# An mLSTM cell followed by a gated two-layer block: a reordered head (later gates, third weighed k, w_in's second quarter, sine's table)

## The chip, the cores and the metric

The kernel runs on one core of a Trainium2 chip. The metric is device time in microseconds (us) of the whole program. The core has five engines that run their own instruction lists in order and wait for one another by semaphores: PE (TensorE, matmul), DVE (VectorE), ACT (ScalarE), POOL (GpSimd) and SP (SyncE, here the engine that issues most DMAs). A profile names an instruction by its line in the kernel ("L528") and its tiles ("qG<-t,G"). Times "at 40.03" are us from the start of the profiled span.

## What is computed

Two stages. The first is an mLSTM cell for 4 batches and 8 heads, 768 steps, head size 40:

```
m_new  = max(f_gate + m, i_gate)
C      = exp(f_gate + m - m_new) * C + exp(i_gate - m_new) * outer(v, k)
n      = exp(f_gate + m - m_new) * n + exp(i_gate - m_new) * k
y[t]   = sigmoid(o_gate) * (C @ q) / max(|n . q|, 1)
```

The second takes the 3072 rows of 320 values that the first gives (8 heads side by side) as x:

```
h   = x @ w_in          (320 x 2048, float64 in memory)
g   = h * cos(h)
out = g @ w_out         (2048 x 320, float64 in memory)
```

All work is in float32. The float64 weights are brought down to float32 in the kernel.

## The kernel before

**Cells.** The sequence is cut into 6 chunks of 128 steps, and a cell n is one chunk of one batch (c, b = divmod(n, 4)), 24 in all. Within a chunk the recurrence is written as a masked product: E holds the decays between two steps (loaded as running maxima from a DRAM table M_d, masked and put through exp), `scores` makes k.q on PE, `weigh` multiplies by E on DVE, `values` multiplies by v on PE. What comes from earlier chunks is a state per batch (`st`), which `values` adds as qG times st, where qG is q scaled by the carry G (loaded by `load_G` or `load_G_of` from a DRAM table G_d). The 4 cells of chunk 0 (n = 0 to 3) have no carry.

**Second stage.** For each chunk c, 8 slots f2 of 256 columns of w_in: `Up(c, f2)` makes h on PE in two PSUM banks "pup" (L725 for the last 64 rows of x, L731 for the other 256), then h*cos(h) by `near` (ACT L739), `rest` (DVE L742), `sin` (ACT L747, which needs the sine table in ACT) and `gate` (DVE L751, tile g). `down` multiplies g by w_out (PE L845, tile po). Up(0, 0) and Up(0, 1) use the first quarter of w_in's columns, Up(0, 2) and Up(0, 3) the second.

**Weights.** A piece of float64 weight comes as pairs of words into a place of the tile `blocks` (w_in: four DMAs L163 of 128 KB, or four L216 of 64 KB for the last rows) or into `bits` (w_out: one DMA L222 of 640 KB). It is brought down by `take_apart` (ACT L175, L177), `bound` (DVE L181, L182), `join` (DVE L191) and `round_up` (POOL L195); `put_together` is the last two. A quarter of w_in is three pieces: two of 512 columns and a last one, w_in_l.

**Order.** The order is written out by hand under a manual schedule: an engine's list is the order of the calls. `first_cells` is the head: the gates, cells 0 to 3, w_in's first quarter and what cell 4 (n = B) needs; `first_period` is slots 0 and 1 of chunk 0 with cell 4; after that `both_parts` runs two slots and one cell at a time. Each engine's list is strictly in order, and so is SP's list of DMA issues. A DMA issue on SP also waits for the landing of the DMA eight issues before it, since eight completion semaphores go round.

**The later gates** (chunks 1 to 5) are made in the head: `gates_sums` (DVE L288), `gates_less_sums` (POOL L291 to L293), `gates_maxima` (DVE scan L296, then POOL issues the DMA to M_d, L298), `gates_exponents` (POOL L301 to L304), `gates_exp` (two ACT exps L308, then POOL issues two DMAs to G_d, L311), `gates_turn` (PE L322, ACT L323 into the table `tab`), `gates_diagonal`, `gates_spread` and `gates_keep` (ACT L332).

**Other places the change touches.** `weigh_k(n)` is POOL L469, k times a gate, into a tile kw of which there are two; cells 2 and 3 reuse the places of cells 0 and 1, which PE reads in `seam` (L683). `load_M(n)` is L424, the masking of E is `decay_exponents` (POOL L450), its exp is `decay` (ACT L464, 8 instructions from cell 4 on). `turn_blocks` (DVE L524) turns q and k for cells from 4 on, `scale_q` is qG (POOL L528), `odd_constants` fills the tile vr (POOL L138, L139) and `odd_values_of` copies a part of v into it (POOL L506). In `values(4)` PE runs, in this order, L572 and L581 (E and qG), again L572 and L581, then L575 and L578 (vr) and L581. `state(n)` copies or adds the state (ACT L706 for n < 4). `warm` gives PE matmuls of zeros.

Of the kernel before, what the change touches and what calls it, by code (L numbers as in the profile page):

```python
# [29 lines left out]
def kernel(  # L30
# [23 lines left out]
    C = 128  # L54
# [138 lines left out]
    def round_up(dst, bits):  # L193
        t = dst.bitcast(I32)
        nc.gpsimd.tensor_tensor(out=t, in0=t, in1=bits[:, 0:dst.shape[1], 0], op=OP.add)  # L195
# [94 lines left out]
    def gates_less_sums():  # L290
        nc.gpsimd.tensor_tensor(out=a1, in0=a1, in1=F1, op=OP.subtract)  # L291
        nc.gpsimd.tensor_copy(out=shift[:, 0, 0:1], in_=F0[:, last])
        nc.gpsimd.tensor_copy(out=shift[:, 1:R, 0:1], in_=F1[:, 0:R - 1, last])  # L293
# [37 lines left out]
    def gates_keep(pd):  # L331
        nc.scalar.copy(out=tab[:, 1:R, 3], in_=pd)  # L332
# [132 lines left out]

    def weigh_k(n):
        if n < N - B:
            kw = p2.tile([128, H, D], FP, name="kw", tag="kw")
            nc.gpsimd.tensor_tensor(out=kw, in0=ks(n)[:, :, 0:D], in1=cols(n, 1, D), op=OP.mult)  # L469
            kws[n] = kw  # L470

# [14 lines left out]
    def turn(n):  # L486

        pool, tag = psum(n)
        pts[n] = []
        for src in (qs(n), ks(n)):  # L490
            pt = pool.tile([128, HP, C], FP, name="pt", tag=tag)
            for p in range(HP):
                nc.tensor.transpose(pt[:, p], pair(src, p), ident)
            pts[n].append(pt)
        qkT[n] = [p1.tile([128, HP, C], FP, name=f"t{i}", tag=f"t{i}") for i in range(2)]
# [58 lines left out]
    def values(n):  # L554
        pool, tag = psum(n)
        E = Es[n]
        if n < B:
            ph = pool.tile([128, H, D1], FP, name="ph", tag=tag)
            for j in range(2):
                for p in range(HP):  # L560
                    h = 2 * p + j
                    nc.tensor.matmul(ph[:, h], E[:, h], vs(n)[:, h, 0:D1], start=True, stop=True)
            heads_of[n] = ph
            return
        vt = pool.tile([128, 4, C], FP, name="vt", tag=tag)
        state = st[n % B]

        for i in range(3):
            if i < 2:
                for a in range(HP):  # L570
                    h = 2 * a + i
                    nc.tensor.matmul(vt[32 * a:32 * a + 32, i], vs(n)[:, h, 0:32], E[:, h], start=True, stop=False)  # L572
            else:
                for a in range(HP):
                    nc.tensor.matmul(vt[32 * a:32 * a + 32, i], vr2[n // 2 % 2][:, n % 2, a, 1:3].rearrange("q g d o -> q (g d o)"),  # L575
                                     E[:, 2 * a + 1], start=True, stop=False)
                for a in range(HP):
                    nc.tensor.matmul(vt[32 * a:32 * a + 16, i], vr2[n // 2 % 2][:, n % 2, a, 0].rearrange("q d o -> q (d o)"),  # L578
                                     E[:, 2 * a], start=False, stop=False)
            for a in range(HP):  # L580
                nc.tensor.matmul(vt[32 * a:32 * a + 32, i], state[:, ts(HP * i + a, 32)], Gs[n][:, a], start=False, stop=True)  # L581
        heads_of[n] = vt
# [502 lines left out]
    def less_sums(n):  # L1085
        for i in range(2):
            decay_exponents_half(n, i)

    def first_cells():
        gates_in()  # L1090
        nc.scalar.copy(out=ident_b, in_=ident)
        for i in range(3):
            r = ts(i, BH)
            nc.scalar.copy(out=of_parts[r], in_=ident[r, r])
        load(0, "qk")
        gates_constants()
        ones_of_values()
        later_gates_in()
        load(0, "v")
        load(1, "qk")  # L1100
        load_o(0)
        load(1, "v")
        load(2, "qk")
        warm(9)
        wall_in(0, 0, pmu)
        gates_first()
        for n in range(B):
            load_E(n)
        load(2, "v")
        load(3, "qkv")  # L1110
        maxima_in_parts()
        gates_first_out()
        wall_in(0, 1, psum_o())
        for i in range(2):
            spread(0, i)
        for i in range(2):
            decay_exponents_half(0, i)
        turn(0)
        turn_out(0, False)
        decay(0)  # L1120
        maxima_in(1)
        less_sums(1)
        weigh_k(0)
        blocks_constants()
        weigh_k(1)
        state_constants()
        scores(0)
        turn(1)
        decay(1)
        turn_out(1, False)  # L1130
        weigh(0)
        sigmoid_next()
        sigmoid(0)
        exp_next()
        gates_sums()
        gates_less_sums()
        values(0)
        pieces.extend(weights_in(0))
        scores(1)
        weigh(1)  # L1140
        maxima_in(2)
        less_sums(2)
        decay(2)
        values(1)
        normalize(0)
        maxima_in(3)
        less_sums(3)
        turn(2)
        turn_out(2, False)
        weigh_k(2)  # L1150
        seam(0)
        gates_maxima()
        gates_exponents()
        load_M(B)
        load_blocks(B)
        load(B, "kv")
        outs.append((0, weights_out(0)))
        load_blocks(B + 1)
        seam_out(0)
        scores(2)  # L1160
        decay(3)
        state(0)
        weigh(2)
        turn(3)
        normalize(1)
        turn_out(3, False)
        weigh_k(3)
        values(2)
        take_apart(*pieces[0])
        seam(1)  # L1170
        normalize(2)
        scores(3)
        seam_out(1)
        bound(pieces[0][0])
        take_apart(*pieces[1])
        seam(2)
        weigh(3)
        values(3)
        join(*pieces[0])
        round_up(*pieces.pop(0))  # L1180
        seam_out(2)
        gates_exp()
        load_G_of(B)
        state(2)
        more = weights_in(1)
        pieces.append(next(more))
        take_apart(*pieces[1])
        normalize(3)
        gates_turn()
        warm(3, psum_o())  # L1190
        bound(pieces[0][0])
        put_together(*pieces.pop(0))
        pieces.append(next(more))
        load_M(B + 1)
        seam(3)
        seam_out(3)
        bound(pieces[0][0])
        put_together(*pieces.pop(0))
        state(1)
        gates_diagonal()  # L1200
        decay_exponents(B)
        pieces.extend(more)
        load_G_of(B + 1)
        load(B + 1, "kv")
        outs.append((1, weights_out(1)))
        load_o(1)
        outs.append((2, weights_out(2)))
        low_dimensions(B)
        turn_blocks(B)
        state(3)  # L1210
        decay(B)
        scale_q(B)
        weigh_k(B)
        odd_constants()
        odd_values_of(B)
# [18 lines left out]
    def first_period():  # L1234
        n = B
        up = Up(0, 0)
        scores(n)
        pd = gates_spread()
        warm(8, psum_o())
        for e in range(2):  # L1240
            up.near(e)
        gates_keep(pd)
        for e in range(2):
            up.rest(e)
        weigh(n)
        for e in range(2):
            up.sin(e)
            up.gate(e)
        values(n)
        seam(n)  # L1250
        p, piece = outs.pop(0)
        take_apart(*piece)
        low_dimensions(n + 1)
        for some in pieces:
            take_apart(*some)
        out_of_psum(n)
        on_vector([piece])
        up = Up(0, 1)
        turn_blocks(n + 1)
        on_vector(pieces)  # L1260
        pieces.clear()
        more = weights_in(2)
        pieces.append(next(more))
        load_M(n + 2)
        pieces.extend(more)
        load_blocks(n + 2)
        load_out(p)
        for e in range(2):
            up.near(e)
        for e in range(2):  # L1270
            up.rest(e)
        for e in range(2):
            up.sin(e)
            up.gate(e)
        p, piece = outs.pop(0)
        take_apart(*piece)
        denominators(n)
        fade(n)
        decay_exponents(n + 1)
        on_vector([piece])  # L1280
        state(n)
        odd_values_of(n + 1)
        down_slot(0, 1)
        sigmoid(1)
        decay(n + 1)
        divide(n)
        scale_q(n + 1)
        weigh_k(n + 1)
        load_G(n + 2)
        load_two(n + 2)  # L1290
        load_out(p)
        load_M(n + 3)
# [257 lines left out]
```

## Time and profile before

| what | value |
|---|---|
| median of 3 runs | 514.73 us (512.44 to 516.18) |
| the profiled execution | 514.64 us, span 512.9 us, so 1.74 us lie around the span |
| granted PE clock, mean | 0.993 |
| busy share | PE 97%, DVE 81%, ACT 63%, POOL 59% |
| PE's gaps over 0.04 us up to 41 us | 0.99, 0.51, 0.13, 0.21, 0.76 us |
| PE's gaps from 41 to 103 us | 0.64, 0.30, 0.54, 0.05, 0.47, 1.39, 0.52, 0.32 us |
| PE's gaps from 103 to 446 us | 0.19, 0.16, 1.06, 1.10, 0.17, 0.26, 0.41, 0.14 us |

How to read it: a line of a timeline has the start, the duration, the engine, the line of code, the operation, the tiles and shapes, and a count where like instructions were merged; in brackets stand the idle time of that engine before it and what ended that wait. A line of the table of stretches has busy time of each engine, then the granted PE clock (1.00 is full), the mean busy share of the 16 DMA engines and what they moved in GB/s. The trace also has the time at which each DMA's completions came in.

### The profile page before, as it was taken

To read this page: it belongs to the slowest core of one execution; us is meant where nothing else is said; L and a number is where in the kernel's file an instruction comes from. 1 tells how busy PE (TensorE), PEld (TensorE's weight loads), DVE (VectorE), ACT (ScalarE), POOL (GpSimd) and SP (SyncE) were. 2 spreads that over 40 slices of the span, in tenths; PEclk is the share of its full clock that TensorE was granted. 3 is DMA by queue.
4 is the path that set the end of the run, shared out by engine and by line. 5 is a ranking of instruction groups with operands and counts; after the bars stand their busy time and mean duration, and the time that the engine had idled before them with its cause. 6 is when DMAs were issued, how large, how long until landed. Compare 5 with 4: busy or idle time off the path is not lost.

```text
span 512.9 us, 11085 instructions
## 1 busy us (share of the span) xinstructions
PE 498.3 (97%) x4034; PEld 376.8 (73%) x4034; DVE 417.6 (81%) x840; ACT 325.2 (63%) x622; POOL 302.8 (59%) x390
## 2 busy tenths in 40 slices
PE   8999998999999999999999999999999999999996
PEld 6765554555675776688888688878778878787876
DVE  7887898986788887889987979998979967677655
ACT  6769779667953657747757858558858654444541
POOL 8443856544825955857576868566767455534340
PEclk9979999999999999999999999999999999999999
DMA  9978989898157527208729106828102000010001
GB/s 136 189 198 197 269 178 279 206 228 164 60 144 140 143 57 151 83 32 189 175 61 186 42 31 169 174 77 174 59 33 82 4 5 6 2 52 0 1 0 54
DMA packets 100583, 56.80 MB, mean 111 GB/s; under 512 B 63472, under 2 KB 93248, under 8 KB 100528
## 3 DMA queue, kind: packets, MB, share of 16 engines
q1 hardware_dynamic: 97408, 54.43, 45.3%
q10 hardware_dynamic: 2752, 1.23, 1.0%
q8 instruction: 32, 0.52, 0.4%
q0 software_dynamic: 368, 0.43, 0.3%
q14 instruction: 23, 0.19, 0.1%
HBM read 50.66 MB, written 4.10 MB: 107 GB/s over the span
## 4 chain that ended last, share of the span: by engine, by line
PE 73%; DVE 8%; DMA 6%; ACT 4%; SPq 3%; POOL 3%; issue 2%; DVEq 0%; ACTq 0%; POOLq 0%
PE acc L995 22%; PE pup L799 16%; PE pup L731 7%; PE pup L815 6%; PE late L995 4%; PE ps L546 4%; PE po L845 3%; PE pup L725 2%; PE vt L581 2%; PE vt L572 2%; DVE t L524 1%; PE pu L683 1%; DMA blocks<-in_moe_w_in_dram 1%; DVE n L742 1%; DMA ks<-in_k_dram 1%
## 5 line engine op out<-in xcount | busy, mean ns | idle before, releaser
L739 ACT ACTIVATE n<-pup 128x512 int32<-128x512 f32 x64 | 37.0, 594 | 95.9 <-DVE pup L824 64.7
L747 ACT ACTIVATE n<-n 128x512 f32<-128x512 f32 x96 | 58.2, 627 | 22.5 <-DVE n L742 16.2
L834 POOL TENSOR_TENSOR g<-g,n 128x512 f32<-128x512 f32 x31 | 39.6, 1276 | 52.2 <-ACT n L747 50.8
L742 DVE SCALAR_TENSOR_TENSOR n<-pup,n 128x512 f32<-128x512 f32 x64 | 43.1, 689 | 23.3 <-ACT n L739 20.8
L731 PE MATMUL pup<-xT,w_in_sb 128*128 128x512 f32 x128 | 59.2, 605 | 2.0 <-DVE g L751 2.0
L995 PE MATMUL acc<-w_out_sb,g 128*128 128x160 f32 x320 | 58.4, 302 | 0.0
L816 POOL TENSOR_TENSOR blocks<-blocks 128x256 f32<-128x256 f32 x32 | 25.7, 802 | 52.4 <-ACT blocks L808 52.4
L995 PE MATMUL acc<-T,g 128*128 128x160 f32 x304 | 55.8, 301 | 0.0
L799 PE MATMUL pup<-xT,w_in_sb 128*128 128x256 f32 x192 | 53.1, 385 | 0.4 <-ACT blocks L808 0.2
L464 ACT ACTIVATE E<-E,tab 128x128 f32<-128x128 f32 x160 | 50.2, 391 | 3.9 <-POOL E L450 3.7
L995 PEld LDWEIGHTS acc<-w_out_sb,g 128*128 128x128 f32 x320 | 49.0, 190 | 4.5 <-issue 2.7
L751 DVE TENSOR_TENSOR g<-pup,n 128x512 f32<-128x512 f32 x64 | 42.6, 687 | 7.5 <-ACT n L747 6.9
L731 PEld LDWEIGHTS pup<-xT,w_in_sb 128*128 128x128 f32 x128 | 23.3, 191 | 33.2 <-issue 31.1
L995 PEld LDWEIGHTS acc<-T,g 128*128 128x128 f32 x304 | 46.0, 190 | 0.9 <-issue 0.4
L799 PEld LDWEIGHTS pup<-xT,w_in_sb 128*128 128x128 f32 x192 | 33.8, 189 | 9.7 <-ACT blocks L808 5.9
L799 PE MATMUL pup<-x_room,room 128*128 128x256 f32 x128 | 38.2, 380 | 0.0
L824 DVE TENSOR_TENSOR pup<-pup,blocks 128x256 f32<-128x256 f32 x32 | 13.9, 436 | 29.2 <-PE pup L815 26.0
L807 ACT COPY blocks<-pup 128x512 f32<-128x512 f32 x32 | 18.6, 580 | 29.5 <-PE pup L799 27.8
L845 PE MATMUL po<-w_out_sb,g 128*128 128x320 f32 x128 | 36.3, 436 | 1.0 <-POOL w_out_sb L195 1.0
L528 POOL TENSOR_TENSOR qG<-t,G 128x512 f32<-128x512 f32 x20 | 25.9, 1295 | 18.7 <-DVE t L524 16.8
L995 PE MATMUL acc<-T,blocks 128*128 128x160 f32 x160 | 36.2, 308 | 0.0
L815 PE MATMUL pup<-xL,w_in_l 64*128 64x512 f32 x128 | 36.1, 641 | 0.0
(219 smaller groups left out, 1219.6 us busy)
## 6 DMA issues: line engine op xcount, KB each, us to landing
E<-M_d SPq DMA_DIRECT2D x20, 512.0 KB
qr<-in_q_dram SPq DMA_DIRECT2D x72, 80.0 KB
kr<-in_k_dram SPq DMA_DIRECT2D x72, 80.0 KB
bits<-in_moe_w_out_dram SPq DMA_DIRECT2D x8, 640.0 KB
G<-G_d SPq DMA_DIRECT2D x18, 256.0 KB
blocks<-in_moe_w_in_dram SPq DMA_DIRECT2D x32, 128.0 KB
out_dram<-o_sb SPq DMA_DIRECT2D x23, 160.0 KB
o<-in_o_gate_dram SPq DMA_DIRECT2D x40, 80.0 KB
```

The costliest lines, as they stand in the source:

```text
L464: nc.scalar.activation(out=Es[n][:, h], in_=Es[n][:, h], func=AF.Exp, scale=-1.0, bias=tab[:, c, 0, g:g + 1])
L528: nc.gpsimd.tensor_tensor(out=qG, in0=qkT[n][0], in1=Gs[n], op=OP.mult)
L731: nc.tensor.matmul(pu.rearrange("p (b t) -> p b t", b=B), w_in_sb[:, i, ts(2 * f2 + e, 128)], xT[c][:, i:NK * B:NK], start=(i == 0 and not ...
L739: nc.scalar.activation(out=self.n[e], in_=self.pu[e], func=AF.Copy, bias=0.25)
L742: nc.vector.scalar_tensor_tensor(out=self.n[e].bitcast(FP), in0=self.pu[e], scalar=0.25, in1=self.n[e], op0=OP.add, op1=OP.subtract)
L747: nc.scalar.activation(out=r, in_=r, func=AF.Sin, scale=TWO_PI_DOWN)
L751: nc.vector.tensor_tensor(out=g, in0=self.pu[e], in1=self.n[e].bitcast(FP), op=OP.mult)
L799: nc.tensor.matmul(bank[:, part].rearrange("p (b t) -> p b t", b=B // 2), w[:, f2], x, start=start, stop=stop, skip_group_check=True)
L815: nc.tensor.matmul(pu, w_in_l[r, f2], xL[c][r].rearrange("p b t -> p (b t)"), start=False, stop=True, skip_group_check=True)
L834: tt(out=self.g, in0=self.g, in1=self.n[e].bitcast(FP), op=OP.mult)
L845: nc.tensor.matmul(po[c][b], gs[c, f][:, ts(b, C)], w_out_sb[:, f], start=(f == 0), stop=(f == NF - 1))
L995: nc.tensor.matmul(a, lhs, rhs, start=start, stop=stop)
```

## The change

Nothing is computed differently; one tile gets another place and calls change their order in the head.

- `weigh_k(2)` writes to a place of its own (the place that o_gate's raw tile has later) and is called right after `gates_less_sums`; before, it came after `turn_out(2)`.
- `gates_maxima` and `gates_exponents` are called before `less_sums(3)`, `turn(2)` and `turn_out(2)`.
- `gates_exp` is called before `seam(2)`; before, it came after `seam_out(2)`, join and round_up of w_in's first piece.
- On SP's list: w_out's second piece (640 KB) is issued right after `load_blocks(B + 1)`; then w_in's second quarter's first two pieces and `load_M(B + 1)`; then `load_G_of(B)`, which before stood ahead of all of these.
- `decay_exponents(B)` comes right after the first piece's round_up, and `bound` of the second piece ahead of `normalize(3)`.
- `state(1)` comes ahead of `seam(3)`; `state(3)` moves from `first_cells` into `first_period`, after `gates_keep`, and `gates_keep` moves from before `rest` to after the two sines.
- `sin_next` (the load of ACT's sine table) is called after `decay(B)`, ahead of `Up(0, 0)`'s nears.

```diff
     def weigh_k(n):
         if n < N - B:
-            kw = p2.tile([128, H, D], FP, name="kw", tag="kw")
+            if n == 2:
+                kw = p1.tile([128, B, 2 * C // 32, D], FP, name="kw_o", tag="o")[:, 0]
+            else:
+                kw = p2.tile([128, H, D], FP, name="kw", tag="kw")
...
         exp_next()
         gates_sums()
         gates_less_sums()
+        weigh_k(2)
         values(0)
...
         normalize(0)
         maxima_in(3)
-        less_sums(3)
-        turn(2)
-        turn_out(2, False)
-        weigh_k(2)
-        seam(0)
         gates_maxima()
         gates_exponents()
         load_M(B)
         load_blocks(B)
+        less_sums(3)
+        turn(2)
+        turn_out(2, False)
+        seam(0)
         load(B, "kv")
         outs.append((0, weights_out(0)))
         load_blocks(B + 1)
+        outs.append((1, weights_out(1)))
         seam_out(0)
...
         take_apart(*pieces[1])
+        gates_exp()
         seam(2)
         weigh(3)
         values(3)
         join(*pieces[0])
         round_up(*pieces.pop(0))
+        decay_exponents(B)
         seam_out(2)
-        gates_exp()
-        load_G_of(B)
         state(2)
         more = weights_in(1)
         pieces.append(next(more))
         take_apart(*pieces[1])
+        bound(pieces[0][0])
         normalize(3)
         gates_turn()
         warm(3, psum_o())
-        bound(pieces[0][0])
+        state(1)
         put_together(*pieces.pop(0))
         pieces.append(next(more))
         load_M(B + 1)
+        load_G_of(B)
         seam(3)
         seam_out(3)
         bound(pieces[0][0])
         put_together(*pieces.pop(0))
-        state(1)
         gates_diagonal()
-        decay_exponents(B)
         pieces.extend(more)
         load_G_of(B + 1)
         load(B + 1, "kv")
-        outs.append((1, weights_out(1)))
         load_o(1)
         outs.append((2, weights_out(2)))
         low_dimensions(B)
         turn_blocks(B)
-        state(3)
         decay(B)
+        sin_next()
         scale_q(B)
...
         for e in range(2):
             up.near(e)
-        gates_keep(pd)
         for e in range(2):
             up.rest(e)
         weigh(n)
         for e in range(2):
             up.sin(e)
             up.gate(e)
+        gates_keep(pd)
+        state(B - 1)
         values(n)
```

## The prediction

> **What bounds the kernel now.** I read the page first, then the timelines of the five engines from 0 to 108 us, SP's waits, and tables of stretches.
>
> ```profile
> PE 498.3 (97%) x4034; PEld 376.8 (73%) x4034; DVE 417.6 (81%) x840; ACT 325.2 (63%) x622; POOL 302.8 (59%) x390
> ...
> PEclk9979999999999999999999999999999999999999
> DMA  9978989898157527208729106828102000010001
> ```
>
> PE carries the time. The DMA engines are 70 to 90% busy in the head (a slice is 12.8 us), and PE's clock falls only there. From 103 us to 446 us PE idles 3.5 us in all, so a change to the head is worth what it moves PE by at about 102 us. What can be won there is PE's idle from 41 to 103 us, 4.2 us, or 0.8%.
>
> ```profile
> 43.33 0.43 PE L572 MATMUL vt<-E,vs 128*32 128x128 f32 x8 [0.64 <-issue]
> 44.34 0.40 PE L575 MATMUL vt<-E,vr 128*32 128x128 f32 x8
> ...
> 79.72 3.67 PE L731 MATMUL pup<-xT,w_in_sb 128*128 128x512 f32 x8 [1.39 <-DVE g L751]
> ...
> 84.98 1.16 PE L546 MATMUL ps<-t,t 40*128 40x128 f32 x16 [0.52 <-DVE t L524]
> ...
> 102.10 3.67 PE L731 MATMUL pup<-xT,w_in_sb 128*128 128x512 f32 x8 [0.32 <-DVE g L751]
> ```
>
> These waits are small and end on DVE: between 45 and 85 us ACT and DVE are nearly as full as PE. ACT's own two waits there are the ones the change aims at, w_in's second quarter and o_gate:
>
> ```profile
> 50.15 0.46 ACT L175 ACTIVATE w_in_l<-blocks 128x256 f32<-128x256 f32 x1 [0.61 <-DMA blocks<-in_moe_w_in_dram]
> ...
> 57.73 1.28 ACT L372 ACT_TABLE_LOAD   x1 [1.68 <-DMA o<-in_o_gate_dram]
> ```
>
> Both come from SP's list, which waits 3.0 us (SP's waits) for G_d ahead of the carry G, while the DMA engines run dry (share 0.15 below):
>
> ```profile
> 31.99 0.86 SPq L393 DMA_DIRECT2D kr<-in_k_dram  x2
> 35.90 1.15 SPq L516 DMA_DIRECT2D G<-G_d  x2
> 37.22 3.71 SPq L163 DMA_DIRECT2D blocks<-in_moe_w_in_dram  x8
> 40.97 0.42 SPq L424 DMA_DIRECT2D E<-M_d  x1
> ```
>
> **The change part by part.**
>
> *Maxima, exponents, third k.* L296 (1.53) starts at 17.4, not 18.62. POOL's 5.47 us wait before L469 goes, so M_d is issued at 19.0 instead of 20.62 and L304 ends at 22.8 instead of 24.38; the fourth k then waits for nothing. M_d landed at 24.64, before SP's issues of w_in_l end at 25.07, so the read of it gains at most SP's wait of 0.3; I take 0. The cost: E(3)'s exp on ACT goes from 19.34 to 20.2, and with it `turn_out(3)` to 23.0; ACT's idle of 1.67 before 23.80 hides it, uncovered it is 0.9.
>
> *Later gates' exps.* L308 (1.36) moves into ACT's idle of 2.00 before 28.68, so `seam_out(2)` is not later. G_d is issued at 27.4, not 30.74, lands near 32, and SP's 3.0 us wait is gone.
>
> *Pieces, mask, sine table.* `bound` (0.9) moves into DVE's idle of 1.56 before 30.92; E(4)'s mask (1.09) into POOL's idle of 2.22 before 34.07. The second round_up ends at 34.4 instead of 35.35, but Up(0, 0) started at 34.35 behind `seam(3)`, of which nothing moves, and did not wait: 0. E(4)'s exp goes from 38.24 to 35.45, the table load (1.28) falls beside Up(0, 0), and near moves from 40.71 to 39.6, so sin, g and the 0.64 wait at 43.33 come 1.1 us sooner or go. `state(3)` (0.75) lands on ACT at 42.4 between sin and w_out's pieces; ACT won 1.1 there, net 0.
>
> *SP's list.* This decides. Behind kr at 32.85 now stand, in order, w_out's second piece (655 KB), eight issues of w_in (1049 KB), E(5) from M_d (524 KB), and only then G for cell 4 (262 KB), which used to be first. Landings come in SP's order in the trace. The rates:
>
> ```profile
> 26.00:28.00 2.00, 2.00 (x18) 1.45 (x16) 1.82 (x4) 0.68 (x2) 0.44 (x1) 0.50 0.86 252
> 35.00:37.00 2.00, 2.00 (x5) 0.76 (x4) 1.93 (x5) 1.79 (x8) 0.93 (x2) 0.93 0.15 41
> 39.00:44.00 5.00, 4.36 (x50) 2.54 (x50) 2.55 (x5) 4.95 (x12) 3.27 (x7) 1.00 0.90 231
> 52.00:54.00 2.00, 2.00 (x9) 1.38 (x8) 2.00 (x4) 0.85 (x2) 1.06 (x1) 1.00 1.04 366
> ```
>
> These are E, the dry stretch, w_in and w_out, in GB/s in the last column. From 35.3, when kr is through: w_out 655/366 = 1.8, w_in 1049/245 = 4.3 (231 here, 258 in the stretch 59 to 64), E 524/260 = 2.0, G 262/260 = 1.0, and 0.4 to the last completion: 44.8. The eighth-before rule does not add: G's two issues go when the second and third w_in pieces have landed, near 40. So w_in_l lands at 46.5 instead of 50 and o_gate near 52 instead of 57.6, and both ACT waits go; but G lands at 44.8 instead of 40.0.
>
> POOL stands at qG with all that is queued behind it:
>
> ```profile
> 40.03 1.27 POOL L528 TENSOR_TENSOR qG<-t,G 128x512 f32<-128x512 f32 x1 [1.82 <-DMA G<-G_d]
> 41.25 0.73 POOL L469 TENSOR_TENSOR kw<-ks,tab 128x320 f32<-128x320 f32 x1
> ...
> 43.17 0.24 POOL L506 COPY vr<-vs 128x64 f32<-128x64 f32 x1
> ```
>
> From qG's start to vr's end are 3.38, say 3.5 with DVE busy beside it. PE, in order, needs qG for L581 and vr for L575: it stands from 42.9 to 46.1 and again to 48.3, where before L575 ran at 44.34. From L575 to the end of Up(0, 1) are 5.84 (44.34 to 50.18), so 54.1 instead of 50.18: 3.9 later. How much survives: from 50.18 to 84.98 PE took 34.80, of it waits 0.30 + 0.54 + 0.05 + 0.47 + 1.39 + 0.52 = 3.3 and some 0.6 in a low product of 1.72 at 67.94 (1.13 elsewhere). Without waits that is 30.9, so 3.9 is given back and PE reaches 84.98's place at 85.0: +0.05. DVE and ACT are not later than that: with 5.84 after 48.3, sigmoid starts 3.4 after PE's end (near, rest, sin 1.95, w_out's take_apart 1.47) at 57.5, against 57.73.
>
> *The clock.* The stall has a second price.
>
> ```profile
> 21.60:25.00 3.40, 2.44 (x30) 2.08 (x31) 3.23 (x11) 1.73 (x4) 2.78 (x4) 1.00 0.86 257
> 25.10:28.40 3.30, 3.30 (x32) 2.65 (x28) 3.02 (x7) 1.57 (x4) 0.93 (x1) 0.50 0.72 211
> 28.50:31.80 3.30, 3.30 (x46) 3.04 (x43) 1.67 (x6) 3.10 (x10) 2.31 (x3) 1.00 0.96 195
> 31.90:35.20 3.30, 3.30 (x26) 1.95 (x24) 2.98 (x7) 1.74 (x8) 1.13 (x1) 0.50 0.91 302
> ```
>
> Stretches of 3.4 us with short matmuls, one of them without a gap, are followed by 3.4 us at half clock. From 42.6 to 49 PE would have about 1.5 us of short matmuls. I take half clock until about 52.3, by when Up(0, 1) has run 3 us: 1.5 us. Bounds: 0 if the clock stays, 3.4 if two stretches of Up and po run at half. The Trainium skill, page "TensorE: Matmul & The Clock Gate", section "The HAM clock gate (the "warmup" mystery)", has the clock fall after an idle window of about 3.4 us; by that the matmuls inside the stall keep it up, and the 1.5 goes (third rival). The row 28.50 to 31.80 disagrees: no idle, and half clock after it.
>
> **Sum.** +0.05 + 1.5 - 0.32 (the wait at 102.10 is absorbed) = +1.2, on the profiled 514.64, which stands 0.09 under the median of the runs: 515.8. With G between 43.9 and 46 and the clock's loss from 0.8 to 2.5 it is 514.2 to 518.
>
> **Rivals.**
>
> *G is not late enough to matter (faster).* If all 2490 KB move at w_out's 366 GB/s, G lands at 35.3 + 6.8 + 0.4 = 42.5, L575 runs at 46.0, PE is 2.25 earlier at 84.98 and the clock may hold: 512.4. For it: w_in rows of 258 at full share, and ACT's slack of 1.68. Against: w_in never ran over 312 in any us of the head. The Trainium skill, page "DMA: Bandwidth & Descriptors", section "Bandwidth", measures 341 GB/s for 1 MB; by it, as an estimate, G's data would be through at 42.6 and the time near this rival's. The w_in rows of 231 and 258 speak against that rate here.
>
> *G is very late (slower by over 1%).* If the stream behind w_out runs at the 163 GB/s of 46 to 50 us, G lands at 35.3 + 1.8 + 1835/163 + 0.4 = 48.8: PE +4.0, clock +1.5, less 0.32: 519.8. It decides from a landing past 48.5. Against: that stretch held 160-byte rows of k and v, which now come after G.
>
> *The stall comes, the clock stays full.* 514.64 + 0.05 - 0.32 = 514.4.
>
> *The change does nothing.* The gates sooner hide behind `seam(3)` and G's delay stays small enough: 514.6, inside the case before.
>
> **How the numbers follow.** Forecast (stall and half clock) 0.53; full clock or nothing 0.18; G early 0.20; G very late 0.06; not foreseen 0.03. A measurement of this kernel tells about 1% (5.1 us) from no change. Over 1% faster (below 509.6) needs G early and half-clock stretches of the head gone as well: 0.04. Over 1% slower (above 519.9): 0.08, the late G and a little. Within: 0.88. The range runs from just below G early, 512.0, to 519.0, leaving out the late G and part of the early one, 0.2 together. The forecast's own range is 514.2 to 518.
>
> **What would show it.** Right: qG starts at 44 to 46 with a wait that ends on DMA G; PE has two gaps in `values(4)`, before L581 and before L575; the clock shows half around 46 to 52; L175 of w_in_l and L372 have no DMA wait; the table load stands before near; PE's L546 at 84.98 comes at 86 to 87. Wrong: qG by 43, or full clock through Up(0, 1), or L546 at 83.

## The result

| kernel | median (us) | runs | ratio to before, 95% interval |
|---|---|---|---|
| before | 514.01 (512.44 to 516.18) | 7 | |
| after | 519.32 (517.51 to 520.32) | 7 | 1.0100 (1.0078 to 1.0122) |

The changed kernel is 5.3 us slower, 1.0%. Its profiled execution took 519.51 us with a span of 517.7 and a mean granted clock of 0.987. PE's timeline of after (start, duration, engine, line, operation, tiles; idle time and its end in brackets; lines past 470 are three higher than in before):

```profile
44.37 0.43 PE L575 MATMUL vt<-E,vs 128*32 128x128 f32 x8
48.76 0.66 PE L584 MATMUL vt<-qG,st 128*32 128x128 f32 x8 [3.96 <-POOL qG L531]
...
51.22 0.65 PE L578 MATMUL vt<-E,vr 128*32 128x128 f32 x8 [0.95 <-POOL vr L509]
...
58.66 4.47 PE L848 MATMUL po<-w_out_sb,g 128*128 128x320 f32 x16
```

```profile
89.56 1.16 PE L549 MATMUL ps<-t,t 40*128 40x128 f32 x16 [0.53 <-DVE t L527]
...
106.71 1.52 PE L734 MATMUL pup<-xT,w_in_sb 128*128 128x512 f32 x3 [0.35 <-DVE g L754]
```

The 0.64 us ahead of the cell's values is gone, and in its place stand two waits on POOL, 3.96 and 0.95 us. The first `down` comes at 58.66 instead of 50.18 (+8.48), the scores of cell 5 at 89.56 instead of 84.98 (+4.58), and from there little changes (106.71 against 102.10, +4.61; +4.87 at the end). The loss arises before 60 us, and a part of it is given back by 90 us.

What PE waits for on POOL is qG, which starts 7.40 us later than in before:

```profile
47.43 1.27 POOL L531 TENSOR_TENSOR qG<-t,G 128x512 f32<-128x512 f32 x1 [9.92 <-DVE w_out_sb L191]
```

The view puts the end of this wait to DVE, whose L191 also ended at 47.43. G's last completion had come at 47.27. In before and in runs 1, 2 and 4 qG started 0.16 to 0.17 us behind G's last completion as well, so I take G for what was waited for.

SP's timeline, and its largest wait from 25 to 46 us (us in total, times, longest):

```profile
33.25 0.43 SPq L222 DMA_DIRECT2D bits<-in_moe_w_out_dram  x1
33.85 7.91 SPq L163 DMA_DIRECT2D blocks<-in_moe_w_in_dram  x8
42.00 0.35 SPq L424 DMA_DIRECT2D E<-M_d  x1
42.49 1.15 SPq L519 DMA_DIRECT2D G<-G_d  x2
```

```profile
SPq L163 <- DMA bits<-in_moe_w_out_dram: 4.5, 2, 2.4
```

The 3.0 us wait for G_d is gone, and two waits for w_out's landings, 4.5 us in all, have come. G is issued at 42.49 and not near 40. The stretches (busy time of PE, PEld, DVE, ACT, POOL, then clock, DMA share, GB/s):

```profile
30.83:37.66 6.83, 4.78 (x28) 2.59 (x26) 5.51 (x14) 3.40 (x14) 3.06 (x3) 0.50 1.03 256
...
44.50:47.90 3.40, 0.29 (x8) 0.02 (x4) 2.86 (x5) 3.25 (x9) 0.47 (x1) 1.00 0.58 160
47.90:54.70 6.80, 4.99 (x68) 3.13 (x68) 5.86 (x9) 3.09 (x7) 4.93 (x8) 0.50 0.69 163
42.00:43.00 1.00, 1.00 (x9) 0.52 (x6) 1.00 (x2) 0.73 (x2) 0.00 (x0) 1.00 0.52 164
```

After a stretch in which PE did nearly nothing (0.29 of 3.40 us), 6.8 us at half clock follow. In the last row the DMA engines stand half idle, just behind the second of SP's waits, which ended at 41.45.

ACT has what was promised to it: the table load stands before near, and w_in_l and the sigmoid have no wait on a DMA.

```profile
39.09 1.28 ACT L1231 ACT_TABLE_LOAD   x1
...
49.75 0.43 ACT L175 ACTIVATE w_in_l<-blocks 128x256 f32<-128x256 f32 x1
...
62.25 1.28 ACT L372 ACT_TABLE_LOAD   x1
```

### The profile page after: what moved, and what is told of

Same layout as the page of the kernel before. It is cut to its first block, busy times and chain, and to the rows that moved or that the text cites. A ratio compares the mean times of both kernels' runs of the same rounds, so it can differ in the third digit from the quotient of the medians.

```text
span 517.7 us, 11083 instructions
## 1 busy us (share of the span) xinstructions
PE 499.8 (97%) x4034; PEld 377.3 (73%) x4034; DVE 418.2 (81%) x840; ACT 325.7 (63%) x623; POOL 302.2 (58%) x390
## 4 chain that ended last, share of the span: by engine, by line
PE 68%; DMA 8%; SPq 7%; DVE 7%; issue 4%; POOL 3%; ACT 3%; ACTq 0%; DVEq 0%; POOLq 0%
PE acc L998 22%; PE pup L802 16%; PE pup L734 6%; PE pup L818 6%; PE late L998 3%; PE ps L549 3%; DMA blocks<-in_moe_w_in_dram 3%; PE po L848 3%; DMA G<-G_d 2%; PE pup L728 2%; PE vt L584 2%; PE vt L575 2%; DMA qr<-in_q_dram 1%; SPq L393 1%; SPq L216 1%
## 5 line engine op out<-in xcount | busy, mean ns | idle before, releaser
L742 ACT ACTIVATE n<-pup 128x512 int32<-128x512 f32 x64 | 37.1, 593 | 104.8 <-DVE pup L827 65.0
L837 POOL TENSOR_TENSOR g<-g,n 128x512 f32<-128x512 f32 x31 | 39.6, 1279 | 52.3 <-ACT n L750 50.9
```

What stands on the lines that cost most here:

```text
L742: nc.scalar.activation(out=self.n[e], in_=self.pu[e], func=AF.Copy, bias=0.25)
L837: tt(out=self.g, in0=self.g, in1=self.n[e].bitcast(FP), op=OP.mult)
```

## The experiments

**Theory:** the loss is G's late landing alone; what is late beyond 3.9 us at the first `down`, the half clock included, reaches the end. **Rivals:** other moved calls cost the time (bound beside POOL's work); w_out's early piece is to blame and not G's own place; the eighth-before waits are; it is the chain from qG to vr. In the table stand the start of qG, of the first matmuls on vr, of the first `down` and of cell 5's scores, each from the profiled execution, and the median of all runs with the ratio to the kernel before on the same chip. The groups of runs come from four chips, on which before took 513.40 to 514.12 us. A profiled execution need not be the median one: in run 5 it took 517.99 us, the least of six.

| run | qG | vr | down | scores | median | ratio (95%) |
|---|---|---|---|---|---|---|
| before | 40.03 | 44.34 | 50.18 | 84.98 | | |
| after | 47.43 | 51.22 | 58.66 | 89.56 | 519.32 | 1.0100 (1.0078, 1.0122) |
| 1 G first | 40.23 | 43.67 | 49.53 | 82.15 | 512.94 | 0.9985 (0.9959, 1.0011) |
| 2 bound back | 47.02 | 50.77 | 59.50 | 90.40 | 519.55 | 1.0091 (1.0060, 1.0123) |
| 3 both | 40.47 | 44.20 | 50.03 | 82.94 | 512.65 | 0.9966 (0.9944, 0.9989) |
| 4 G late in before | 46.14 | 50.46 | 58.80 | 89.67 | 519.18 | 1.0105 (1.0077, 1.0132) |
| 5 SP's list in before | 45.85 | 49.77 | 57.28 | 88.17 | 520.23 | 1.0131 (1.0105, 1.0156) |
| 6 more zeros | 46.95 | 51.31 | 57.17 | 88.04 | 518.71 | 1.0084 (1.0054, 1.0114) |
| 7 w_out back | 45.27 | 49.19 | 57.36 | 88.27 | 518.30 | 1.0092 (1.0066, 1.0117) |
| 8 mask later | 41.35 | 45.88 | 53.38 | 84.27 | 513.66 | 0.9995 (0.9976, 1.0014) |
| 9 G in the middle | 41.45 | 45.97 | 51.83 | 82.91 | 516.19 | 1.0037 (1.0008, 1.0067) |
| 10 G before E(5) | 46.01 | 49.76 | 57.59 | 88.46 | 517.63 | 1.0073 (1.0047, 1.0099) |
| 12 all early | 40.01 | 44.51 | 50.34 | 83.58 | 512.70 | 0.9976 (0.9954, 0.9997) |
| 13 vr first | 45.84 | 48.95 | 55.72 | 86.63 | 517.99 | 1.0075 (1.0046, 1.0104) |
| 15 G in the middle, vr first | 43.28 | 46.03 | 51.86 | 84.80 | 513.56 | 0.9996 (0.9976, 1.0017) |

### 1 to 3: is it G, or the other moves?

```diff
# 1: after, with
         take_apart(*pieces[1])
         gates_exp()
+        load_G_of(B)
...
         load_M(B + 1)
-        load_G_of(B)
# 2: after, with (3 has both edits)
-        bound(pieces[0][0])
         normalize(3)
         gates_turn()
         warm(3, psum_o())
+        bound(pieces[0][0])
         state(1)
```

> The kernel after with one call moved: the two reads of G for cell 4 go on SP's list right behind w_out's second piece, ahead of w_in's second quarter and E(5); all else as in after. Theory (the late G is the whole loss): G lands near 38 to 40 us instead of 47.3, qG is no longer the last to be waited for at the cell's values, the gaps of 3.96 and 0.95 us in PE and the half clock from 47.9 to 54.7 go; 519.3 - 3.7 (the stall's net at the scores of cell 5 without the clock's part, 4.6 - 1.6 = 3.0, and the 0.64 us gap won) - 1.6 (clock), with up to 1.1 us lost again because the late start of Up(0, 0) is no longer hidden: 513 to 516. Rival (the other moves cost the time): 517.5 or more, with the two gaps gone.

> The kernel after with bound of w_in's second piece put back behind normalize(3) and the turn of the gates. Theory (PE stands for qG at 48.8 us whatever is ready before): DVE's L182 is short again (0.4 us instead of 2.86), Up(0, 0) starts about 1 us sooner, and the time stays within 0.5 us of 519.3, since the wait for qG is 1 us longer. Rival (the slow bound on DVE beside POOL's work is a loss of its own): 518.2.

> Both edits: G's reads ahead of w_in's second quarter, and bound in its old place. Theory: with the stall for qG gone the late start of Up(0, 0) is no longer covered, so this is about 1 us below the run with G first alone, 512 to 515. Rival (DVE's collision is covered elsewhere, by ACT's w_in_l or by sin): the same time as with G first alone within 0.4 us.

One moved call takes back the whole loss: 512.94 instead of 519.32, just under the range that I gave. POOL still waits for G in it, but only to 40.23, and in the cell's values PE waits for nothing:

```profile
40.23 1.27 POOL L531 TENSOR_TENSOR qG<-t,G 128x512 f32<-128x512 f32 x1 [4.40 <-DMA G<-G_d]
```

```profile
42.57 0.43 PE L575 MATMUL vt<-E,vs 128*32 128x128 f32 x8
...
43.67 0.42 PE L578 MATMUL vt<-E,vr 128*32 128x128 f32 x8
```

The rest of the change is worth about -0.3%: with G first and bound in its old place the ratio is 0.9966, with an interval (0.9944 to 0.9989) just under 1. Bound alone (2) changes nothing that can be measured, as the theory had it. That run 3 would be 1 us below run 1 did not come: 0.29 us, inside the noise. In it PE still waits 1.53 us for y, which run 8 looks into.

### 4, 5, 7: is it G's place, or w_out's piece ahead of it?

```diff
# 4: before, with
         gates_exp()
-        load_G_of(B)
...
         load_M(B + 1)
+        load_G_of(B)
# 5: as 4, and outs.append((1, weights_out(1))) where after has it
# 7: after, with
         load_blocks(B + 1)
-        outs.append((1, weights_out(1)))
...
         load(B + 1, "kv")
+        outs.append((1, weights_out(1)))
```

> The kernel before with one call moved: the two reads of G for cell 4 stand on SP's list behind w_in's second quarter and E(5); w_out's second piece stays where before has it. Theory (G's landing follows the bytes ahead of it, and w_out's piece adds about 4 us to them in after): G lands near 43.2 us (35.3 + 1835 KB / 245 GB/s + 0.4), qG starts at 43.3 instead of 40.03, the vr matmuls at 46.9 instead of 44.34; 2.5 us of stall, given back before the scores of cell 5, and 0 to 1.5 us of clock: 514.0 to 516. Rival (G at this place is as late as in after, w_out's piece does not matter): qG at 46 or later, 517 to 519.

> The kernel before with the whole order of after on SP's list (w_out's second piece early, G for cell 4 behind w_in's second quarter and E(5)) and nothing else of the change. Theory (the list is the whole loss): qG at 46.5 to 48, the stall and the half clock of after, 518.5 to 520. Rival (part of the loss comes from the other moves): 515.5 to 518.

> The kernel after with w_out's second piece put back on SP's list to its place of before, behind k and v of cell 5; G stays behind w_in's second quarter and E(5). Theory (w_out's piece ahead of G costs 4 us: its 655 KB and the wait for its last completion): G lands at 43.2, qG at 43.4, the vr matmuls at 47.0 instead of 51.22, po near 53 instead of 58.66; that is given back, and the clock's price is 0 to 1.5: 513 to 515.5. Rival (w_in and E(5) are what holds G, w_out's piece adds little): qG at 46 or later, 517 to 519.

Run 5 confirms that SP's list alone makes the loss (520.23). Runs 4 and 7 went against me: without w_out's 655 KB ahead of it, G's last completion still came at 45.97 and 45.12, and the time stayed at 519.18 and 518.30. What is ahead of G in all three is w_in (1049 KB) and E(5) (524 KB), and the start of that stream was later than I had it: kr's last completion came at 37.45 (run 4) and 37.40 (run 7), not at 35.3. The bytes of w_out do show in the first 12 of the 16 engines: they were through G at 44.19 and 43.85, against 46.52 in after. But the last engine came 1.78 and 1.27 us behind them, against 0.75 in after, and qG waits for the last.

### 9 and 10: how late may G be?

```diff
# 9: after, with load_G_of(B) behind the first of w_in's two pieces
         pieces.append(next(more))
+        load_G_of(B)
         take_apart(*pieces[1])
...
         load_M(B + 1)
-        load_G_of(B)
# 10: after, with
-        load_M(B + 1)
         load_G_of(B)
+        load_M(B + 1)
```

> The kernel after with the two reads of G for cell 4 on SP's list behind w_out's second piece and the first of the two pieces of w_in's second quarter (four of the eight issues); the second piece and E(5) come behind. Theory (the time follows the landing of the last of G's two reads, which follows the bytes ahead of it): G lands 2.2 us behind where it landed with G first (40.07), at about 42.3, qG at 42.4, the last vr matmuls wait to about 46 instead of 51.22; that lies within what the stretch to 85 us gives back, so 513 to 515, 1 to 2 us above the run with G first. Rival (any G behind w_in is as bad as after): 518 or more.

> The kernel after with G's two reads ahead of E(5) on SP's list, behind all of w_in's second quarter's eight issues. Theory: E(5)'s 524 KB took 1.95 us from landing to landing, so G lands at 45.0 to 45.4 instead of 47.27, qG at 45.4, the vr matmuls at 49.2 instead of 51.22, and the time falls by 1.5 to 2.0 us to 517.3 to 517.8 (more if a half-clock stretch goes). Rival (SP's waits for the eighth-before set G, not the bytes): G is issued at 42.0 instead of 42.49 and lands at most 0.5 us sooner, 518.8.

Run 10 came out as the bytes have it: qG 1.42 us sooner, 1.7 us less time, although G's last completion (45.85) missed the 45.0 to 45.4. Run 9 has qG at 41.45, sooner than expected, and yet 516.19. Its profile shows a wait of 2.33 us on vr and no half clock behind it; that profiled run took 512.60 us, the second lowest of the twelve. Five of the others, at a mean clock of 0.986, took 516.7 to 517.9.

### 13 and 15: the chain behind qG

```diff
# 13: after, with (15: the same in run 9)
         sin_next()
+        odd_constants()
+        odd_values_of(B)
         scale_q(B)
         weigh_k(B)
-        odd_constants()
-        odd_values_of(B)
```

> The kernel after with vr's constants and the copy of v into it ahead of qG on POOL, where POOL stands idle for 9.9 us. Theory (PE waits once for qG at 48.8, then again 0.95 us for vr): the second gap goes, the last vr matmuls run at 49.6 to 50.3 instead of 51.22, and since the stretch to 85 us has nothing more to give back, the time falls by 0.9 to 1.6 us, 517.7 to 518.4. Rival (vr's wait is covered by the half clock or by ACT and DVE, which are late anyway): 519.0 or more.

> The run with G behind the first piece of w_in's second quarter, with vr's constants and copy ahead of qG on POOL. Theory (there it is the chain of 4.5 us from qG to vr, not G's landing at 41.4, that holds PE for 2.33 us and, with the half clock that follows in most runs, makes 516.2 of 512.9): the gap of 2.33 goes, the runs at a mean clock of 0.986 go with it, and the time is 512.2 to 513.2. Rival (G's landing at 41.4 is late enough by itself): 515 or more.

Run 13 has the time that was expected, 517.99, and the 0.95 us wait is gone. The vr matmuls run at 48.95, sooner than the 49.6 to 50.3, since G landed at 45.33 in that profile. From qG's start to them are 3.11 us instead of 3.79; how much of the 1.3 us in the median is vr's place and how much is G is not shown. In run 15 the median is 0.4 us above what I gave it, no run has a mean clock under 0.989, and vr makes no one wait, although qG started at 43.28, 1.83 us later than in run 9. So G's landing at 41.4 is not late by itself. In run 9 the chain from qG to vr takes 4.5 us (41.45 to 45.91; 3.73 in after): the two memsets of L139 (0.43 instead of 0.20 each) and the copy (L509, 0.86 instead of 0.58) were slower there, beside DVE's `bound` and `join` of w_out. That this chain costs run 9 its 2.6 us by way of the clock is likely and not shown: the two profiled executions reach `down` at the same time (51.83 and 51.86), since run 15's had lost 2.75 us to a wait on y before Up(0, 0), and what sets the medians apart lies in runs without a profile.

### 6: the clock

```diff
         pd = gates_spread()
-        warm(8, psum_o())
+        warm(28, psum_o())
```

> The kernel after with 28 instead of 8 matmuls of zeros ahead of the cell's values, so that PE is not idle while it waits for qG (the 20 more fill about 4 us and nothing is left out of the computation). Theory (the half clock from 47.9 to 54.7 us is the price of the idle stretch from 44.5 to 47.9, 1.6 us): PE's clock stays at full through Up(0, 1) and the time is 1.0 to 1.6 us below after, 517.7 to 518.3. Rival (the clock falls after short matmuls too, as it did at 25 to 28 us in the kernel before): half clock all the same, and 519.3 or up to 0.5 more.

```profile
43.38 6.22 PE L1080 MATMUL pm<-room 128*128 128x512 bf16 x28
49.52 0.43 PE L575 MATMUL vt<-E,vs 128*32 128x128 f32 x8
...
52.57 1.13 PE L728 MATMUL pup<-xL,w_in_l 64*128 64x512 f32 x4
53.63 3.70 PE L734 MATMUL pup<-xT,w_in_sb 128*128 128x512 f32 x8
```

With the stall filled the clock stays full in that stretch: L728 takes 1.13 us where after took 1.74. From L578 to `down` it is 5.86 us and not 7.44, and the scores of cell 5 come 1.52 us sooner. The median fell by 0.6 us only, and its interval (1.0054 to 1.0114) overlaps that of after; the term is shown in the profile, not by the times.

### 11 and 14: the eighth-before waits

```diff
# 11: after, each of w_in's second quarter's pieces in one DMA over [4, 32, 1024 words]
...
+            if f == 1:
+                bits = bits_tile()
+                nc.sync.dma_start(out=bits.rearrange("p n two -> p (n two)"), in_=w_in_rows[:, D * i:D * i + 32, ts(f, 2 * WP)])
...
# 14: both pieces in four DMAs, each over [32, 2, 1024 words]
...
+        for a in range(HP):
+            nc.sync.dma_start(out=both[32 * a:32 * a + 32], in_=rows[a, 0:32, :, 2 * WP:4 * WP])
...
```

> The kernel after with each 512 KB piece of w_in's second quarter in one DMA instead of four of 128 KB: the same rows and bytes, but six issues fewer ahead of E(5) and G, so that neither waits for a landing eight before. Theory (the waits for the eighth-before add, about 0.8 us of DMA time between 41 and 44 us in after): G is issued by 36 and lands at 46.2 to 46.6 instead of 47.27, and the time falls by 0.7 to 1.1 us, 518.2 to 518.6. Rival (the waits are hidden, the data ahead and the engines that lag set the landing): 47.0 to 47.5 and 519.3 within 0.4. A landing before 46 would say that the waits cost more than the idle DMA time shows.

> The kernel after with w_in's second quarter's two pieces read in four DMAs of 256 KB instead of eight of 128 KB, over the same 16 engines, same bytes in the same place of SP's list. The issues of E(5) and G then wait for landings before w_out's second piece, not for it. Theory A (the waits for the eighth-before add): G is issued by 39 to 40, the DMA engines do not run dry at 42 to 43 us, G lands 0.6 to 1.2 us sooner, at 46.1 to 46.7, and the time falls by 0.6 to 1.2 us to 518.1 to 518.7. Theory B (they do not; the bytes ahead and lagging engines set the landing): G lands at 47.0 to 47.6, 519.3 within 0.4.

Neither says anything of the waits. In run 11 (524.99 us, ratio 1.0216, 1.0183 to 1.0249) a DMA with an outermost size of 4 reported from 4 of the 16 engines, and w_in crawled: a DMA share of 0.28 and 109 GB/s from 44 to 53 us. The Trainium skill, page "DMA: Bandwidth & Descriptors", section "Why a DMA increments its semaphore by 16 and not by 1", says that the number of engines used must divide the size of the slowest dimension; the four completions agree. Run 11 does show the loss going on: qG 6.15 us later than in after, 5.7 us more time. Run 14 (526.31, ratio 1.0249, 1.0219 to 1.0279; not all of w_in's second quarter gets to its place in it) held PE for 12.43 us ahead of Up(0, 0): ACT and DVE stood until 45.29 for a DMA, 15.81 and 11.97 us, waits that my edit made.

What the waits cost can be read from the runs that share after's list on SP. The landings come from the trace:

| run | w_out's last completion | G's last completion | DMA share 42 to 43 us |
|---|---|---|---|
| 13 | 38.59 | 45.33 | 0.99 |
| 5 | 39.01 | 45.68 | 0.99 |
| 2 | 39.32 | 46.86 | 1.01 |
| 6 | 39.98 | 46.79 | 1.04 |
| after | 41.43 | 47.27 | 0.52 |

Where w_out is complete by 40 us, the eighth w_in issue comes while the engines still have work, and the wait is hidden. In the profiled after it came at 41.45, and the engines were 0.84, 0.52 and 0.88 busy from 41 to 44 us: 0.76 us of idle time in all. What that did to G is taken up behind the experiments.

### 8 and 12: DVE beside POOL, and the best order

```diff
# 8: run 3, with
         round_up(*pieces.pop(0))
-        decay_exponents(B)
         seam_out(2)
...
         put_together(*pieces.pop(0))
+        decay_exponents(B)
# 12: run 8 with G ahead of w_out's second piece and vr first
```

> The third experiment (G first, bound in its old place) with the mask of E(4) moved from right behind the first round_up to right behind the second one. Theory (DVE's operations on SBUF stand still while POOL's round_up and mask run back to back, 29.6 to 31.9 us, so that y of cell 3, 2.35 us instead of 0.56, holds PE for 1.53): y takes 0.56 to 1.2 us, PE's gap before px of cell 3 shrinks to under 0.6, Up(0, 0) starts about 1 us sooner, and the time falls by 0.3 to 1.0 us below the third experiment's, what is left being taken back by the waits on g and w_out at 60 and 77 us. Rival (y waits for something else, the clock's state or its own inputs): y and the gap stay as they are.

> The kernel of the fourth group's last run (G early, bound in its old place, the mask of E(4) behind the second round_up) with G's two reads ahead of w_out's second piece, and with vr's constants and copy ahead of qG on POOL. Theory: G lands near 38 instead of 41.2, vr is ready by 39, so the three gaps of 0.26, 0.56 and 2.33 us before the cell's values shrink to at most 0.3 in all while Up(0, 0) still starts near 33.1; 1 to 2 us below the run with the mask later, 511.5 to 512.7. Rival (what is won at the head is taken back by the waits on w_out at 60 and g at 77 us): 512.6 to 513.5.

In after, DVE's L182 stood while POOL ran two operations with no gap between them:

```profile
29.29 2.86 DVE L182 TENSOR_SCALAR w_in_sb<-w_in_sb 128x512 int32<-128x512 int32 x1
```

```profile
29.51 1.31 POOL L195 TENSOR_TENSOR w_in_sb<-w_in_sb,blocks 128x512 int32<-128x512 int32 x1
30.77 1.09 POOL L450 TENSOR_SCALAR_AFFINE_SELECT E<-E 128x1024 f32<-128x1024 f32 x1
```

In run 3 it is y (L643, 2.35 us instead of 0.56) that stands there. With the mask moved away (run 8) y took 0.85, the bound behind it was short, PE's wait of 1.53 was gone and Up(0, 0) started at 33.09 instead of 34.21:

```profile
30.37 0.85 DVE L643 TENSOR_TENSOR y<-room,dn 128x256 f32<-128x256 f32 x2
31.15 0.41 DVE L181 TENSOR_SCALAR w_in_sb<-w_in_sb 128x512 f32<-128x512 f32 x1
```

The Trainium skill, page "SBUF — State Buffer", section "Who interferes with whom", says that of such a pair of operations the one that issues first holds the shared port pair for its whole length and the other stands. Here the DVE operation stood through both of POOL's, from 29.72 (when 0.43 would have ended it) to 32.15, although by the recorded starts it was first (29.29 against 29.51); in that the trace differs. The mechanism was right, the gain was not: G's last completion came at 41.20 in run 8 (40.31 in run 3), vr was ready only at 45.83, and PE waited 2.33 there. Run 12 takes those waits to 0.22 and is at 512.70, not to be told from run 3. In its profile nothing was won before 50 us: PE waited 1.77 us before 16.10, ahead of anything that sets this run apart from run 3, Up(0, 0) started at 35.10 and not near 33.1, and `down` came at 50.34 (50.03 in run 3). So whether a gain there would be taken back by the waits on w_out and g at 61 and 78 us (0.73 and 1.39) is not shown.

## Why the prediction was wrong, point by point

*The step that failed* is G's landing: "From 35.3, when kr is through" and the sum to 44.8. Measured was 47.27, 2.47 us later. By the completions of the first 12 of the 16 engines, w_out's piece was through at 38.96 and not at 37.1, and these 1.86 us have three parts. I had read 35.3 from the mean busy share, but in before 12 engines were through kr at 36.02 and the last at 36.82 (0.72). In after 12 engines were through kr at 36.85 and the last at 38.69 (0.83 more). And w_out took 2.11 and not 1.8 (0.31). From there w_in took 4.51 (4.3 predicted), E 1.97 (2.0) and G 1.08 (1.0), and the last engine came 0.75 behind (0.4), 0.61 more in all. The other runs with after's list on SP had G's last completion at 45.33 to 46.86, so after's own profile is the latest of the five. The 312 GB/s that I gave as w_in's most in the head is not what the rows show: by whole us it is 294 in 23 to 24, and 333 in 44 to 45, where w_in's end and E overlap. The sum did not use it.

*"The eighth-before rule does not add"* is open. G's issue came at 42.49 and not near 40, and the engines had 0.76 us of idle time. But w_in was not longer for it: by the first 12 engines it took 4.50, 4.46, 4.36 and 4.51 in runs 2, 5, 6 and 13, which had no such idle time, and 4.51 in after. E behind it took 1.97 in after and 1.40, 1.57, 1.51 and 1.44 there, so for most engines the wait probably cost 0.4 to 0.6 us, which my 2.0 for E covered by luck. For the last engine it is doubtful: w_in's seventh piece was complete only at 44.39, long after the eighth was issued at 41.45, so an engine that lagged still had work.

*The sum.* The first `down` was to be 3.9 + 1.5 = 5.4 us late and was 8.48. Of the 3.1 missing, qG's start is 2.63 (47.43 against 44.8), the chain to L578 0.29 (3.79 against 3.5), the clock 0.1.

*What is given back* held to a tenth: 8.48 - 4.58 = 3.90 against 3.9. The amount is the same in all runs of the table whose `down` came over 3 us late: runs 2, 4, 5, 6, 7, 8, 10 and 13 give 3.90, 3.93, 3.91, 3.93, 3.89, 3.91, 3.93 and 3.89. My forecast without the clock used up all of it, so each further us of delay came through whole. The rival "very late" put the landing from which the loss passes 1% at 48.5; after lost 1.0% with G at 47.27.

*The clock* held: from L578 to `down` 7.44 us against 5.84 before, 1.6 instead of 1.5. In a rival I had let the clock stay full, thinking that short matmuls would lie inside the stall. They did not; PE was idle from 44.80 to 48.76, and half clock came from 47.90 on. The Trainium skill, page "TensorE: Matmul & The Clock Gate", section "The HAM clock gate (the "warmup" mystery)", has half clock follow an idle window of about 3.4 us, and here the trace agrees, as run 6 does.

*The 0.32 at 102.10* was to be absorbed and was not: 0.35 stands at 106.71. So 514.64 + 4.61 = 519.25, against 519.51 measured.

*Right:* the gates' steps brought nothing; G_d was issued sooner (28.38; 27.4 was forecast) and SP's wait of 3.0 is gone; w_in_l and the sigmoid have no wait on a DMA; the 0.64 is closed.

*Wrong and covered:* `bound` "in DVE's idle" was not free (L182 alone took 2.86 us, where 0.9 stood for L181 and L182), Up(0, 0) started at 35.47, not 34.35, and near at 41.33, not 39.6. In after the wait for qG hides it. L296 started at 18.42, not 17.4, and M_d went at 20.26, not 19.0; nothing waits for either.

*Left open:* what the eighth-before waits cost, for want of a run that changes them and nothing else; why kr was later in after than in before; and how much the half clock is worth in the median, where its stretches move from run to run.

## What to carry to other kernels

Ask of each transfer in a strictly ordered queue who waits for it and when; put the small one that the bound engine needs soon ahead of the large ones that are needed late, even where the queue must stand a moment for it. When a forecast uses up the slack that gives a delay back, every further error comes out in full: the range must then reach out on that side. Start a landing sum from the last engine's completion of what is ahead, not from the mean busy share: from kr's 36.82 in before, the same sum gives 46.3 instead of 44.8.

## What the runs showed of the hardware that was not expected

- The 16 engines of a DMA can end far apart. w_out's second piece in after was done on 12 engines by 38.96, and on the last four at 39.54, 39.74, 40.86 and 41.43. A wait on its semaphore is a wait for the slowest: SP's issue behind it came at 41.45.
- Two operations on POOL with no gap between them held one DVE operation through both (2.86 us instead of 0.43).
- The mean clock differs from run to run of one kernel. The profiled before has two stretches of 3.41 us at half clock before 40 us and a mean of 0.993; by that, 0.985 would be four or five (an estimate). Of the 26 runs of before beside runs 1 to 3 and 6, the six at a mean clock of 0.985 to 0.989 took 515.8 to 516.3, and five of the six at 1.000 took 511.7 to 512.3 (the sixth took 515.8).
- Half clock from 30.83 in after follows 3.41 us in which PE was busy for 3.38, mostly with short matmuls, and had no gap over 0.03 us, so an idle stretch is not the only thing that brings it.
